# Attention stage of a fused attention and gated-MLP kernel: maxima in bursts next to P times V, a longer lag of ScalarE behind VectorE, and v copied by one engine

## The chip, the cores and the metric

The kernel runs on one core of one Trainium2 chip. The metric is the device time of one execution in microseconds; of the kernel before there are three runs, with a median of 1105.15 us (1102.87 to 1105.18). One further execution was profiled; it took 1106.79 us, 1.6 us over that median. A core has a matrix engine (TensorE; PE in the profile, with its weight loads listed as PEld), VectorE (DVE), ScalarE (ACT), GpSimd (POOL), and SyncE (SP), which here only starts DMA transfers. Each engine works through its own instructions in order and waits on semaphores for the others.

## The reference

One layer norm feeds two branches, and both are added to the input. The first branch is causal attention with 32 heads of 20 columns and a sliding window of 256 keys over 2048 tokens; the second is a gated MLP with 1728 hidden columns.

```python
xn = layernorm(x)                                  # 2048 x 640
q, k, v = split(xn @ wqkv)                         # 32 heads x 20
s = (q @ k.T) * 20 ** -0.5                         # masked: 0 <= row - col < 256
attn = softmax(s) @ v @ wo
mlp = (gelu_tanh(xn @ w_gate) * (xn @ w_up)) @ w_down
out = x + attn + mlp
```

## The kernel before

All dense products are made from numbers that are split in a high and a low part, three matrix multiplications for one (`dense_steps`, L100 to L106). The program has three stages. In the first one the layer norm is computed and x is transposed. In the second one, `attention()` (L753), all of the attention is computed while dense products run between its parts. The third stage holds the rest of the gate and up products and the down and output projections; the change does not touch it.

The attention stage has 32 units: 8 groups of 4 heads times 4 chunks of 512 query rows (`u = g * 4 + c`). Each unit has 14 slots, and `now[0]` counts slots. The order in which the five engines get their work is written out by hand in that loop (a manual schedule for PE, ACT, DVE and POOL); only the order of the SP queue, which starts most DMAs, is left to the framework. Within a unit these parts are issued:

- Eight calls of `max_pair` (L456). A call computes 128 query rows against up to 384 keys for two heads at once; the two heads use two halves of the rows of the matrix engine and write two PSUM banks (`ps_m`, tag `mx`). VectorE then reduces each bank to row maxima (L475). A burst is `pull_max(2, T)`: two calls, four banks, four reductions. The bursts run ahead: with twelve calls made before unit 0, a burst in unit u works for unit u+1 or u+2. `MXD` slots after the last call of a unit, `max_end` (L489) transposes the maxima (`ps_n`) and sends them to the q tile as two further rows.
- Twelve calls of `exp_piece` (L516): scores of one head into a bank of the pool `psx` (`ps_e`, tag `ex`, two banks), which ScalarE turns into exponentials `P` (L532). Two calls are made every other slot. After each fourth call POOL clears the corners outside of the mask (`clear`, L536).
- One call of `av_unit` for the unit before (L549): P times v for four heads in four column groups of the matrix engine, 1536 columns for each head and 1152 in chunk 0, into one bank (`ps_o`) that ScalarE copies to `ob` (L561).
- In slot 12, `load_stack(u + 3)` (L442): twelve DMAs that bring the q and k of a later unit.
- In every slot, `pull_fill(RATE / NS)`: 42.2 / 14 = 3.01 dense matmuls as fill between the rest. They make the q and k projections (`proj_qk`), the v projections (`proj_v`), and six tiles of the gated MLP (`gate_up_fill`), one after another.

A projection that has ended is taken out of its PSUM bank in steps, each deferred by slots (`defer`). For q and k (`save_qk`): ScalarE copies the high part (`upper`), VectorE subtracts (`middle`, L254), ScalarE copies the rest (`lower`, L239), POOL subtracts once more (L240), and a slot later SP stores. For the MLP: `c1` (ACT), `c2` (DVE, L610), `c3` (ACT, tanh, L614), `c4` and `c5` (DVE), and a store. VectorE steps of this kind go through `late()`: they are collected, and `flush()` issues them behind the other work of the slot. For v (`save_v`, L307): four copies from one bank, two by ScalarE and two by VectorE in turn while the attention loop runs.

PSUM has eight banks: two for fill (`psd`), two for scores (`psx`), and four (`psm`) for maxima, `ps_n`, and, before the change, `ps_o`.

Of the kernel before, what the change touches and what calls it, by code (L numbers as in the profile page):

```python
# [9 lines left out]
F32 = mybir.dt.float32  # L10
F32R = mybir.dt.float32r
BF = mybir.dt.bfloat16
AF = mybir.ActivationFunctionType
# [6 lines left out]
C = 512  # L20
# [10 lines left out]
NS = 14  # L31
RATE = 42.2
V1_SLOT = 158
MXD = 6
BURSTS = 1, 5, 9, 13
NFA = 6
HD = D // 2
HR = 5
# [26 lines left out]
def block_kernel(ctx, tc, x, wqk, wv, wgu, wdo, wdl, out):  # L65
    nc = tc.nc
# [65 lines left out]
    psx = pp.enter_context(tc.tile_pool(name="psx", bufs=2, space=PSUM))  # L132
    psm = pp.enter_context(tc.tile_pool(name="psm", bufs=4, space=PSUM))
# [71 lines left out]
    def flush():  # L205
        while lates:
            fn, a = lates.pop(0)
            fn(*a)

    def defer(n, fn, *a):  # L210
        if now[0] is None:
            fn(*a)
        else:
            at(now[0] + n, fn, *a)
# [17 lines left out]
    def save_qk(t, c, ps):  # L232
        pt = qkp.tile([128, 3, C], BF, name="pt", tag="pt")
        r = qkp.tile([128, C], F32, name="r", tag="r", bufs=1)
        dst = (qd if t < 5 else kd)[c]
        h, l = (2, 0) if t < 5 else (0, 2)

        def lower():
            nc.scalar.activation(pt[:, 1, :], r, AF.Copy)  # L239
            nc.gpsimd.tensor_tensor(out=pt[:, l, :], in0=r, in1=pt[:, 1, :], op=OP.subtract)  # L240
            defer(1, store)

        def store():
            a, end = t % 5 * 128, t % 5 * 128 + 128
            while a < end:
                g, b = divmod(a, 4 * DH)
                n = min(4 * DH - b, end - a)
                p = n - end + a + 128
                nc.sync.dma_start(dst[g, :, b:b + n, :].rearrange("p m t -> m p t"), pt[p - n:p])
                a += n  # L250
            done.add((t, c))

        def middle():
            nc.vector.tensor_tensor(out=r, in0=ps, in1=pt[:, h, :], op=OP.subtract)  # L254
            defer(1 if now[0] is None or now[0] < NS else 2, lower)

        def upper():
            nc.scalar.activation(pt[:, h, :], ps, AF.Copy)
            late(middle)

        defer(1, upper)
# [45 lines left out]
    def save_v(ps, vt, t):  # L307
        done.update((id(v), t) for v in vt)
        for g in range(4):
            o = vt[g][:, t * 84:(t + 1) * 84].rearrange("p (j d) -> p j d", d=21)[:, :, 0:20]  # L310
            i = ps[:, g * 80:(g + 1) * 80].rearrange("p (j d) -> p j d", d=20)
            if g % 2 and now[0] is not None:
                nc.vector.tensor_copy(o, i)  # L313
            else:
                nc.scalar.activation(o, i, AF.Copy)

    def run(*gens):
        for gen in gens:
# [197 lines left out]
    def exp_piece(u, s):  # L516
        g, c = divmod(u, NC)
        bi, j = divmod(s, 4)
        bank = pieces(c)[bi]
        q = qs[u % NQ]  # L520
        if j == 0:
            pts[u, bi] = ap.tile([128, 4, C], F32, name="P", tag="P", bufs=3)
        pt = pts[u, bi]
        lo = min(p[1] for p in bank)
        hi = max(p[1] + p[3] for p in bank)
        ps = psx.tile([128, C], F32, name="ps_e", tag="ex")
        for kb, col, q0, n in sorted(bank, key=lambda p: p[3]):
            k = ks[(u - (kb < 4 * c)) % NK]
            kc = kb % 4 * 128
            nc.tensor.matmul(ps[:, col:col + n], k[0:QROWS, j, kc:kc + 128], q[0:QROWS, j, q0:q0 + n],  # L530
                             start=True, stop=True)
        nc.scalar.activation(pt[:, j, lo:hi], ps[:, lo:hi], AF.Exp, scale=SCALE)  # L532
        if j == 3:
            defer(1, clear, u, bi)
# [13 lines left out]

    def av_unit(u):  # L549
        g, c = divmod(u, NC)  # L550
        o, v = psm.tile([128, C], F32, name="ps_o", tag="mx"), vtiles[g]
        todo = [(pts[u, bi], *p) for bi, bank in enumerate(pieces(c)) for p in bank]
        for i, (pt, kb, col, q0, n) in enumerate(todo):
            assert (id(v), kb) in done, (u, kb)
            for j in range(4):
                w0_ = kb * 84 + 21 * j
                nc.tensor.matmul(o[32 * j:32 * j + 32, q0:q0 + n], v[:, w0_:w0_ + 32], pt[:, j, col:col + n],  # L557
                                 start=i == 0, stop=i == len(todo) - 1, skip_group_check=True,
                                 tile_position=(0, 32 * j))
        ob = ap.tile([128, C], F32, name="ob", tag="ob", bufs=1)  # L560
        nc.scalar.activation(ob, o, AF.Copy)  # L561

        def store():
            for j in range(4):
                nc.sync.dma_start(od[c].rearrange("(d h) t -> h d t", h=H)[4 * g + j], ob[32 * j:32 * j + DH, :])
            nc.sync.dma_start(sd[c][4 * g:4 * g + 4, :], ob[DH::32, :])

        defer(3, store)
# [27 lines left out]
    def gate_up_fill(f, ws, c):  # L596
        cs = slice(c * C, (c + 1) * C)
        pss = []
        st = {}

        def c1():
            gs = st["g"] = hp.tile([128, C], F32, name="gs", tag="gs")
            t = st["t"] = hp.tile([128, C], F32, name="he", tag="he", bufs=2)
            nc.scalar.activation(gs, pss[0], AF.Copy)
            nc.scalar.activation(t, pss[0], AF.Square, scale=math.sqrt(0.044715))
            defer(1, late, c2)

        def c2():
            gs, t = st["g"], st["t"]
            nc.vector.scalar_tensor_tensor(t, t, 1.0, gs, op0=OP.add, op1=OP.mult)  # L610
            defer(2, c3)

        def c3():
            nc.scalar.activation(st["t"], st["t"], AF.Tanh, scale=math.sqrt(2.0 / math.pi))  # L614
            defer(1, late, c4)

        def c4():
            nc.vector.scalar_tensor_tensor(st["g"], st["t"], 1.0, st["g"], op0=OP.add, op1=OP.mult)
            st["done"] = True

        def c5():
            if "done" not in st:
                defer(1, late, c5)
                return
            nc.vector.scalar_tensor_tensor(st["t"], st["g"], 0.5, pss[1], op0=OP.mult, op1=OP.mult)
            defer(1, lambda: nc.sync.dma_start(hd[f][c], st["t"]))

        for i, (wh, wl) in enumerate(ws):
            ps = psd.tile([128, C], F32, name="ps_d", tag="dn")
            pss.append(ps)  # L630
            yield from dense_steps(ps, lambda k: wh[:, k, :], lambda k: wl[:, k, :],
                                   lambda k: xh[:, k, cs], lambda k: xl[:, k, cs], KT)
            defer(1, *((late, c5) if i else (c1,)))
# [101 lines left out]
    def pull_max(n, slot):  # L735
        for _ in range(n):
            x = next(stream, None)
            if x is None:
                return
            max_pair(*x)  # L740
            if x[1] == 7:
                at(slot + (MXD if slot >= 0 else 4), max_end, x[0])
# [10 lines left out]
    def attention():  # L753
        now[0] = -1
        load_stack(0)
        load_stack(1)
        load_stack(2)
        for i, (p, k, half) in enumerate((p, k, half) for p in range(NC // 2) for k in range(2) for half in range(2)):
            for j, fn in enumerate(x_sums(p, k, half)):
                at(XS0 + XSN * i + 2 * j, fn)  # L760
        for i in range(12):
            now[0] = i - 13
            for fn, a in tick():
                fn(*a)
            if i % 2 == 0:
                pull_max(2, now[0])
            flush()
            pull_fill(2 * RAMP)
        pull_fill(GAP)
        for u in range(NU + 1):  # L770
            for i in range(NS):
                T = now[0] = NS * u + i
                for fn, a in tick():
                    fn(*a)
                if i == 0 and u:
                    av_unit(u - 1)
                if i % 2 and i < 12 and u < NU:
                    exp_piece(u, i - 1)
                    exp_piece(u, i)
                if i in BURSTS:  # L780
                    pull_max(2, T)
                flush()
                if i == 12 and 3 <= u + 3 < NU:
                    load_stack(u + 3)
                pull_fill(RATE / NS)
        while acts:
            now[0] += 1
            for fn, a in tick():
                fn(*a)
            flush()  # L790
        now[0] = None
        run(fill)
        assert not acts
# [651 lines left out]
```

## Time and profile before

| what | us |
|---|---|
| median of three runs | 1105.15 |
| profiled execution, whole | 1106.79 |
| its span on the core | 1105.0 |
| before unit 0 begins, about | 95 |
| units 0 to 31 and the last P times V | 579 |
| the rest | 431 |
| TensorE busy over the span | 1075.9 |
| VectorE busy over the span | 755.6 |
| ScalarE busy over the span | 512.6 |

The middle three rows are stretches of the profiled span (0 to 95, 95 to 674 and 674 to 1105 us). Busy time of TensorE counts modelled durations that overlap, so for TensorE the starts of its instructions say more than the busy share: in a row of the timeline the first column is the start of a merged group, and the difference to the start of the next row is what the group really took. The idle time in brackets is what was left after the modelled end.

### The profile page before, as it was taken

The numbers are of one execution on the slowest core, as the hardware profiler recorded it, in microseconds if no ns is written. First come the engines' busy times: TensorE is split into PE (matmuls) and PEld (weight loads), VectorE is DVE, ScalarE is ACT, GpSimd is POOL, SyncE is SP. The second block draws the span as 40 slices with busy tenths as digits, with TensorE's granted clock in tenths as the row PEclk, the third lists the DMA queues.
The fourth block names the chain that finished last, engine by engine and source line by source line (L and its number), as shares of the span: only waits on it lengthen the run. The fifth ranks groups of instructions, "written<-read, shape, count | busy, mean of one in ns | idle before, by whom it ended". The sixth has DMA issues, their size and how long they took to land.

```text
span 1105.0 us, 21154 instructions
## 1 busy us (share of the span) xinstructions
PE 1075.9 (97%) x7253; PEld 823.8 (75%) x7253; DVE 755.6 (68%) x2033; ACT 512.6 (46%) x1040; POOL 335.8 (30%) x514
## 2 busy tenths in 40 slices
PE   8999999999999999999999999999999999999998
PEld 7977565556666756666656657888888999999998
DVE  7755566556565556676666744777776869888887
ACT  4434565556544455546455556422323544433332
POOL 5022563557653265535436322111110000000000
PEclk9999999999999999999999999999999999999999
DMA  5552343454543244243424214457666883344443
GB/s 205 169 157 64 98 142 96 127 149 142 166 124 91 67 119 147 91 132 96 128 78 130 90 45 151 161 207 257 230 206 238 296 277 102 121 136 127 133 132 107
DMA packets 105171, 158.45 MB, mean 143 GB/s; under 512 B 15420, under 2 KB 60092, under 8 KB 105064
## 3 DMA queue, kind: packets, MB, share of 16 engines
q1 hardware_dynamic: 102680, 150.95, 43.0%
q10 hardware_dynamic: 2384, 6.16, 1.7%
q8 instruction: 57, 0.93, 0.4%
q14 instruction: 50, 0.41, 0.1%
HBM read 101.78 MB, written 54.92 MB: 142 GB/s over the span
## 4 chain that ended last, share of the span: by engine, by line
PE 59%; DVE 5%; ACT 2%; issue 1%; DMA 1%; POOL 1%; ACTq 0%; SPq 0%; DVEq 0%; POOLq 0%
PE ps_g L894 16%; PE ps L1161 15%; PE ps_d L104 14%; PE ps_o L557 5%; PE ps_e L530 4%; PE ps_m L471 2%; PE ps_v L104 2%; PE ps_g L104 1%; DVE junk L475 1%; DMA hr<-hd 1%; DVE at L999 1%; DVE ss L999 1%; DVE wb L999 1%; DVE wt L999 1%; ACT P L532 1%
## 5 line engine op out<-in xcount | busy, mean ns | idle before, releaser
L475 DVE CUSTOM_DVE_ANT_0 junk<-ps_m,mask 128x384 bf16<-128x384 f32 (+2 forms) x512 | 272.7, 533 | 190.0 <-PE ps_m L471 133.5
L532 ACT ACTIVATE P<-ps_e 128x512 f32<-128x512 f32 (+2 forms) x384 | 197.8, 569 | 68.0 <-PE ps_e L530 66.2
L1161 PE MATMUL ps<-wb,at 128*128 128x320 f32 x999 | 157.0, 310 | 2.2 <-DVE at L999 1.3
L1161 PEld LDWEIGHTS ps<-wb,at 128*128 128x128 f32 x999 | 148.9, 188 | 3.6 <-DVE at L999 1.8
L543 POOL TENSOR_SCALAR_AFFINE_SELECT P<-P 128x512 f32<-128x512 f32 x128 | 85.6, 669 | 183.3 <-ACT P L532 173.4
L104 PE MATMUL ps_d<-xh,wql 128*128 128x512 f32 x430 | 132.7, 416 | 0.0
L104 PE MATMUL ps_d<-xh,wqh 128*128 128x512 f32 x430 | 131.1, 414 | 0.8 <-DVE v L313 0.8
L104 PE MATMUL ps_d<-xl,wqh 128*128 128x512 f32 x430 | 131.2, 412 | 0.0
L530 PE MATMUL ps_e<-qs,ks 124*128 124x128 bf16 (+2 forms) x704 | 113.7, 277 | 10.5 <-ACT P L532 9.3
L104 PEld LDWEIGHTS ps_d<-xh,wqh 128*128 128x128 f32 x430 | 76.7, 189 | 28.4 <-issue 13.6
L104 PEld LDWEIGHTS ps_d<-xh,wql 128*128 128x128 f32 x430 | 77.5, 190 | 25.7 <-issue 13.0
L104 PEld LDWEIGHTS ps_d<-xl,wqh 128*128 128x128 f32 x430 | 77.6, 189 | 25.4 <-issue 12.6
L530 PEld LDWEIGHTS <-ks 124*128 124x128 bf16 x704 | 50.9, 98 | 60.6 <-issue 47.2
L1161 PE MATMUL ps<-wt,at 128*128 128x320 f32 x552 | 89.2, 310 | 0.8 <-DVE xr L1184 0.8
L557 PE MATMUL ps_o<-P,v 128*32 128x384 f32 (+2 forms) x1408 | 84.5, 386 | 2.0 <-DVE mx L475 1.0
L1161 PEld LDWEIGHTS ps<-wt,at 128*128 128x128 f32 x552 | 82.9, 188 | 1.3 <-DVE xr L1184 1.0
L546 POOL TENSOR_SCALAR_AFFINE_SELECT P<-P 128x512 f32<-128x512 f32 x112 | 71.2, 646 | 27.2 <-ACT P L532 27.2
L240 POOL TENSOR_TENSOR pt<-r,pt 128x512 bf16<-128x512 f32 x40 | 46.5, 1163 | 106.7 <-ACT pt L239 104.3
L1115 ACT ACTIVATE at<-ss 128x512 fp32r<-128x512 f32 x59 | 37.3, 632 | 88.7 <-DVE ss L999 88.7
L557 PEld LDWEIGHTS ps_o<-P,v 128*32 128x32 f32 x1408 | 40.6, 110 | 41.8 <-issue 26.9
L561 ACT ACTIVATE ob<-ps_o 128x512 f32<-128x512 f32 x32 | 19.1, 598 | 102.5 <-PE ps_o L557 71.9
L471 PE MATMUL ps_m<-ks,qs 60*128 60x128 bf16 (+1 forms) x704 | 63.5, 275 | 1.9 <-DVE xl L188 1.0
(190 smaller groups left out, 1687.3 us busy)
## 6 DMA issues: line engine op xcount, KB each, us to landing
hr<-hd SPq DMA_DIRECT2D x104, 128.0 KB
hd<-he SPq DMA_DIRECT2D x50, 256.0 KB
wr<-wgu SPq DMA_DIRECT2D x27, 320.0 KB
qs<-qd SPq DMA_DIRECT2D x64, 120.0 KB
ks<-kd SPq DMA_DIRECT2D x64, 120.0 KB
xi<-x SPq DMA_DIRECT2D x16, 320.0 KB
qs<-qd SPq DMA_DIRECT2D x64, 80.0 KB
ks<-kd SPq DMA_DIRECT2D x64, 80.0 KB
```

The lines of the kernel that those rows point to most:

```text
L104: nc.tensor.matmul(ps, a(k), b(k), start=n == 0, stop=n == 3 * nk - 1)
L240: nc.gpsimd.tensor_tensor(out=pt[:, l, :], in0=r, in1=pt[:, 1, :], op=OP.subtract)
L471: nc.tensor.matmul(ps[:, lo:hi], q[rows, j, 128 * b:128 * b + 128], kt[rows, j, k0:k1], start=True, stop=True, tile_position=(64 * r, 0))
L475: nc.vector.tensor_tensor_reduce(out=junk[:, 0:n], in0=ps[:, 0:n], in1=mask[:, 384 - n:384], scale=1.0, scalar=NEG, op0=OP.add, op1=OP.max ...
L530: nc.tensor.matmul(ps[:, col:col + n], k[0:QROWS, j, kc:kc + 128], q[0:QROWS, j, q0:q0 + n], start=True, stop=True)
L532: nc.scalar.activation(pt[:, j, lo:hi], ps[:, lo:hi], AF.Exp, scale=SCALE)
L543: nc.gpsimd.affine_select(out=a, in_=a, pattern=[[0, 4], [1, 128]], compare_op=OP.is_ge, fill=0.0, base=0, channel_multiplier=-1)
L546: nc.gpsimd.affine_select(out=a, in_=a, pattern=[[0, 4], [-1, 128]], compare_op=OP.is_ge, fill=0.0, base=-1, channel_multiplier=1)
L557: nc.tensor.matmul(o[32 * j:32 * j + 32, q0:q0 + n], v[:, w0_:w0_ + 32], pt[:, j, col:col + n], start=i == 0, stop=i == len(todo) - 1, ski ...
L894: nc.tensor.matmul(ps, i, j, start=first and n == 0, stop=n == len(work) - 1, skip_group_check=True)
L999: nc.vector.tensor_tensor(out=o, in0=i, in1=j, op=op)
L1161: nc.tensor.matmul(ps[bank][:, 0:HD], *work[bank][j], start=bank not in begun, stop=final[p, bank] == n and j == len(work[bank]) - 1, skip ...
```

## The change

Four things change in the attention loop.

- The bursts move from slots 1, 5, 9 and 13, behind the scores of the slot, to slots 0, 4 and 8, ahead of them. Slot 0 has two bursts, one ahead of `av_unit` and one behind it, with a `flush()` between. In unit 0, which has no `av_unit`, the second burst is in slot 2.
- The scores move from the odd slots 1 to 11 to the even slots 0 to 10.
- `ps_o` moves from the pool `psm` to `psx`, and so takes a turn with the banks of the scores.
- `lower` follows `middle`, and `c3` follows `c2`, by `LAG = 4` slots and no longer by 2. The four copies of `save_v` are all made by ScalarE.

```diff
-BURSTS = 1, 5, 9, 13
+LAG = 4
...
         def middle():
             nc.vector.tensor_tensor(out=r, in0=ps, in1=pt[:, h, :], op=OP.subtract)
-            defer(1 if now[0] is None or now[0] < NS else 2, lower)
+            defer(1 if now[0] is None or now[0] < NS else LAG, lower)
...
-            if g % 2 and now[0] is not None:
-                nc.vector.tensor_copy(o, i)
-            else:
-                nc.scalar.activation(o, i, AF.Copy)
+            nc.scalar.activation(o, i, AF.Copy)
...
-        o, v = psm.tile([128, C], F32, name="ps_o", tag="mx"), vtiles[g]
+        o, v = psx.tile([128, C], F32, name="ps_o", tag="ex"), vtiles[g]
...
-            defer(2, c3)
+            defer(LAG, c3)
...
+                if i in (0, 4, 8) or T == 2:
+                    pull_max(2, T)
                 if i == 0 and u:
                     av_unit(u - 1)
-                if i % 2 and i < 12 and u < NU:
-                    exp_piece(u, i - 1)
+                    flush()
+                    pull_max(2, T)
+                if i % 2 == 0 and i < 12 and u < NU:
                     exp_piece(u, i)
-                if i in BURSTS:
-                    pull_max(2, T)
+                    exp_piece(u, i + 1)
                 flush()
```

## The prediction

> **What bounds the kernel now.** I read the busy shares by stretch first, then the waits of TensorE and of ScalarE, and then the timeline of TensorE row by row.
>
> ```profile
> span 1105.0 us, 21154 instructions
> ```
>
> ```profile
> 95.00:674.00 579.00, 563.59 (x4267) 357.68 (x4265) 351.11 (x1178) 312.51 (x643) 290.24 (x460) 1.00 0.37 111
> 674.00:1105.00 431.00, 424.66 (x2440) 390.19 (x2432) 342.31 (x669) 163.50 (x294) 19.05 (x13) 1.00 0.55 183
> ```
>
> The columns are the stretch, busy time of PE, PEld, DVE, ACT and POOL, granted clock, DMA share, GB/s. In the attention stretch PE is busy for 563.6 of 579 us at full clock, DVE for 351 (61%), ACT for 313: TensorE bounds it. It can only get shorter by stalls that go away and by matmuls that take less time. The second stretch is not edited and I take it as it is.
>
> ```profile
> PE ps_e L530 <- ACT P L532: 9.3, 13, 0.9
> PE ps_v L104 <- DVE v L313: 2.4, 3, 1.1
> PE ps_d L104 <- DVE v L313: 0.8, 1, 0.8
> ```
>
> ```profile
> ACT pt L239 <- DVE r L254: 26.0, 22, 2.8
> ACT he L614 <- DVE he L610: 20.6, 13, 3.1
> ```
>
> These are us in total, times, longest. Nearly all that PE waits for here are score banks which ScalarE has not emptied, and v banks. The next rows, three engines in one stretch, show why.
>
> ```profile
> 118.66 0.56 DVE L475 CUSTOM_DVE_ANT_0 junk<-ps_m,mask 128x384 bf16<-128x384 f32 x1 [1.62 <-PE ps_m L471]
> ...
> 119.36 0.56 DVE L475 CUSTOM_DVE_ANT_0 junk<-ps_m,mask 128x384 bf16<-128x384 f32 x1
> ...
> 121.13 1.08 PE L104 MATMUL ps_d<-xl,wqh 128*128 128x512 f32 x4
> 121.27 0.69 DVE L254 TENSOR_TENSOR r<-ps_d,pt 128x512 f32<-128x512 f32 x1
> ...
> 121.99 0.63 ACT L239 ACTIVATE pt<-r 128x512 bf16<-128x512 f32 x1 [2.31 <-DVE r L254]
> 122.52 2.19 ACT L532 ACTIVATE P<-ps_e 128x512 f32<-128x512 f32 x4
> 123.15 0.86 PE L530 MATMUL ps_e<-qs,ks 124*128 124x256 bf16 x4 [0.95 <-ACT P L532]
> 123.95 0.52 PE L471 MATMUL ps_m<-ks,qs 60*128 60x128 bf16 x8
> 124.32 0.56 DVE L475 CUSTOM_DVE_ANT_0 junk<-ps_m,mask 128x384 bf16<-128x384 f32 x1 [2.08 <-PE ps_m L471]
> 124.40 0.50 PE L104 MATMUL ps_d<-xl,wqh 128*128 128x512 f32 x1
> ```
>
> Four reductions, 0.71 us apart (118.66 to 119.36), hold DVE for 2.8 us; `middle` (L254) stands behind them. `lower` (L239) comes two slots later at the head of ACT's queue, waits 2.31 us for `middle`, and behind it stand the exponentials, so PE waits for a score bank.
>
> **Prices on TensorE**, from starts:
>
> ```profile
> 415.86 0.61 PE L530 MATMUL ps_e<-qs,ks 124*128 124x128 bf16 x4
> 416.17 1.00 PE L104 MATMUL ps_d<-xh,wqh 128*128 128x512 f32 x3
> 417.01 0.85 PE L104 MATMUL ps_d<-xh,wql 128*128 128x512 f32 x3
> 417.70 0.61 PE L530 MATMUL ps_e<-qs,ks 124*128 124x256 bf16 x4
> 418.24 0.50 PE L471 MATMUL ps_m<-ks,qs 60*128 60x128 bf16 x8
> 418.68 0.73 PE L104 MATMUL ps_d<-xh,wql 128*128 128x512 f32 x2
> 419.25 1.09 PE L104 MATMUL ps_d<-xl,wqh 128*128 128x512 f32 x4
> ...
> 420.92 1.33 PE L104 MATMUL ps_d<-xh,wqh 128*128 128x512 f32 x5
> 422.17 0.50 PE L471 MATMUL ps_m<-ks,qs 60*128 60x384 bf16 x4
> 422.60 0.96 PE L104 MATMUL ps_d<-xh,wql 128*128 128x512 f32 x3
> 423.75 2.80 PE L557 MATMUL ps_o<-P,v 128*32 128x384 f32 x48 [0.19 <-DVE mx L475]
> 426.48 0.73 PE L104 MATMUL ps_d<-xh,wql 128*128 128x512 f32 x2
> 427.05 0.40 PE L104 MATMUL ps_d<-xl,wqh 128*128 128x512 f32 x1
> ```
>
> - One fill matmul takes 0.23 us (three from 417.01 to 417.70).
> - Two scores take 0.31 us to the next fill, which then has 0.15 us more than three times 0.23: 0.46 in all. That is 0.45 ns for each of 1024 columns, the rate of the fill: entering and leaving scores is free.
> - A burst costs 0.10 us ahead (five fills took 1.25 and not 1.15), 0.43 itself, and 0.11 behind (two fills took 0.57): 0.64. Its 768 columns (two pairs, each side by side) stream in 0.35 at that rate. So 0.29 is entry (0.10) and exit (0.19). Behind scores it costs no less: 417.70 to 418.68 and 0.11 is 1.09, minus 0.46 is 0.63.
> - P times v takes 2.73 and 0.11 behind it; its entry, not readable beside the 0.19 of idle time, I take as 0.10.
>
> **The change, part by part.**
>
> *Order on PE.* Before, a unit has five such passages (four bursts and P times v) with an entry and an exit each: 5 x 0.29 = 1.45 us. After, slot 0 has one entry, burst to P times v (a), P times v to burst (b), and an exit to scores (c); slots 4 and 8 each an entry and an exit to scores. That is 0.30 + a + b + 3c. None of the three stands in the trace. For c, the exit to fill is the bound above (0.19); it has 0.08 ahead of the fill and 0.11 behind its first matmul, and 0.08 alone is the bound below; 0.15, between them, since scores leave for free otherwise. For a and b, the bounds are nothing and a whole exit and entry (0.29); the nearest row is the entry alone, 0.10. So 0.95, and 0.50 saved per unit; 0.45 taken. Full bursts fall in 30 units: **-14 us**, between 0 and -27.
>
> The row has 0.10 in and 0.19 out of each passage. The Trainium skill, "TensorEngine Tiling (Array Packing)", Key Properties, says that changing the tiling mode drains TensorE. The two heads of a burst and the four of P times v are different modes, so by that rule a and b are whole changes and this term is near its small end; the rival of cheap joins below is that case.
>
> *LAG.* For about 30 q and k projections `lower`, its subtraction on POOL and two or three stores on SP come two slots later; for 24 gate tiles c3 comes two slots later, and c4, c5 and the store one. Two slots hold six fills and two scores, 6 x 0.23 + 0.46 = 1.84 us, more than the 1.36 that PE lost in the stretch above (worked out next). So both ACT rows above should nearly vanish, and the 13 PE waits with them. Their price is more than the 0.72 of idle time: from 121.13 to 123.15 four fills took 2.02 and not 0.93, and scores and burst (123.15 to 124.40) 1.25 and not 0.98, so 1.36 there. At 1.15 each: **-15 us** (-10 to -18). What it costs: `middle` writes `r` again one slot after `lower` of the set before (sets are 15 / 3.01 = 5 slots apart), so DVE may wait for POOL. That is covered by the idle part of DVE except where it falls into slots 12 and 13, ahead of the maxima.
>
> *v by ACT alone.*
>
> ```profile
> L315 ACT ACTIVATE v<-ps_v 128x80 f32<-128x80 f32 x80 | 16.4, 241 | 45.5 <-DVE v L313 26.5 <-PE ps_v L104 18.7 <-issue 0.2
> L313 DVE COPY v<-ps_v 128x80 f32<-128x80 f32 x48 | 11.4, 240 | 15.3 <-ACT v L315 15.2
> ```
>
> The two engines alternate and wait for each other. 48 copies of 0.24 move: 11.4 us more on ACT, which loses 26.5 of waiting. The four PE waits (3.2 us, with refill about 4) go; new ones behind exponentials cost perhaps 1: **-3 us** (0 to -4).
>
> *ps_o in psx.* ACT's copy frees the bank about 0.7 us after P times v; the burst behind it and the first score take 0.43 + 0.23. Nothing, or 0.1 x 31 at the worst.
>
> *New waits in slot 0.* The second burst needs the four banks of the first. Its reductions begin 0.37 after the burst (123.95 to 124.32): 0.10 + 0.37 + 4 x 0.71 = 3.31 us after the slot begins. PE gets to the last two banks at 0.10 + 0.43 + 2.73 + 0.17 = 3.43: just hidden. In eight units P times v is short (1152 of 1536 columns, 0.68 less), and PE waits about 0.55: **+4 us**. Where a VectorE step of slot 13 comes late, the wait is up to 0.7; seven such units: **+4 us** for this and the `r` case (0 to 20; the upper end is one step of 0.69 in each of 30 units).
>
> *Loads.* A unit's q and k are loaded from slot 12 on; the first maxima that need them stood 11 slots later and now 6. From the prices, slots 0 to 3 take 4.84, 0.69, 1.15 and 0.69: slot 4 begins 7.4 us after slot 0, 6.8 after P times v starts.
>
> ```profile
> 276.13 1.07 PE L557 MATMUL ps_o<-P,v 128*32 128x384 f32 x16
> ```
>
> ```profile
> 441.54 0.16 PEld L557 LDWEIGHTS ps_o<-P,v 128*32 128x32 f32 x8 [0.36 <-POOL P L543]
> ```
>
> ```profile
> 277.20 3.29 SPq L450 DMA_DIRECT2D qs<-qd  x6
> 280.53 2.21 SPq L450 DMA_DIRECT2D ks<-kd  x6
> ...
> 439.99 3.00 SPq L450 DMA_DIRECT2D ks<-kd  x6
> ```
>
> ```profile
> 0.81 1.82 SPq L137 DMA_DIRECT2D xi<-x  x4
> 3.98 0.49 DVE L142 BATCH_NORM_STATS2 st<-xi 128x6 f32<-128x320 f32 x1 [2.86 <-DMA xi<-x]
> ```
>
> At the program's start a transfer was usable 3.2 us after its issue began, which I use as flight. The last of the six issues from 280.53 begins at about 282.4 and then lands at 285.6, 9.5 us after P times v began at 276.13: 2.7 late for slot 4. Most units are like the other one: its last issue begins at about 442.6 and lands at 445.8, 4.3 us after P times v began at 441.54 and 2.5 early. With four or five late units of 30, taken as missing by 1 us each, as the scores end a slot earlier and free the q tile for the load: **+4 us** (0 to 30).
>
> Sum: -14 - 15 - 3 + 4 + 4 + 4 = -20 us. The span of 1105.0 would be about 1085; against the profiled execution 1106.8 that is 1087, against the median, 1.6 lower, **1085**. 0.2% (2.2 us) is about what a measurement can tell from no change.
>
> **The rivals.**
>
> - *Joins are not cheap* (a and b 0.29 each, c 0.15): the order saves 0.12 x 30 = 4 us and no longer 14, so 1095. For it: each change of shape that the trace shows costs. Against: the 0.19 of an exit is partly the fill's own weight load, which neither join has. 0.17.
> - *VectorE becomes late*: eight reductions (5.7 us) stand in slot 0 of a unit that is to take 17.5, and 0.69 late in every unit costs 30 x 0.69 = 21 and not 4: 1102. For it: 16 reductions of 0.71 and 4.2 MLP steps of 0.69 are 14.3 of 17.5 us. Against: slots 9 to 13 have none of the maxima, and five slots of fill to catch up. 0.10.
> - *The loads bind* (slower): the place is the first weight load of the burst in slot 4, which waits for twelve DMAs. In the order of the SP queue of the changed program a store that waits for POOL or VectorE stands between the twelve in 18 units, against 7 before. Each microsecond by which an average unit's loads miss slot 4 costs 30. The rest of the sum is -24, so it decides from 0.8 us on; at 1.1 it gives 1114. For it: one unit as quoted misses by 2.7. Against: these stores belong to slots before 13, and the typical unit has 2.5 us to spare. 0.13.
> - *The lag does nothing*, since ACT then waits in other places: 15 us less gain, 1100. Only where DVE is over 4 slots late, which the second rival has: within its chance.
>
> **How the numbers follow.** The sum has 0.60, with a range of its own from 1071 (joins free, loads in time) to 1096. With 0.17, 0.10 and 0.13 for the three rivals, 1066 to 1107 leaves out the loads' case and the far ends. Faster: 0.60 + 0.17 and half of the second, 0.82 less 0.02 for ends = 0.80; within 0.2%: 0.05; slower: 0.13 and 0.02.
>
> **What would show it.** In the profile after, the last P times v starts near 651 and no longer at 671. The PE waits for `P` fall under 3 us, ACT's waits for `r` and `he` under 10 together. A start-to-start reading of slot 0 gives a, b and c. The order is wrong if burst, P times v, burst and two scores take over 4.9 us without a wait; the loads' rival is right if the weight load of L468 waits for q or k DMAs for over 10 us; VectorE's if PE waits for `mx` or `junk` for over 15.

## The result and the profile after

The changed kernel takes **1079.51 us** (median of 4, 1077.33 to 1081.88) against 1105.16 for the kernel before beside it (1102.87 to 1107.01): a ratio of 0.977, interval 0.974 to 0.980, 25.6 us less. It was forecast faster, at 1085. The profiled execution took 1078.76 us.

Three marks divide the gain in the two profiled spans (1105.0 and 1076.7). The first P times v starts at 110.53 before and at 107.74 after, 2.8 earlier. From the first to the last P times v it is 561.0 us before and 537.0 after; I call this **the loop**, and it lost 24.0. What follows the last P times v was 433.5 and is 431.9. Of the first 2.8, 1.7 is a clock dip that fell into the profile of before alone (last section).

The span and the attention stretch of after, by windows (columns as in the prediction):

```profile
span 1076.7 us, 21130 instructions
95.00:653.00 558.00, 547.91 (x4269) 365.02 (x4269) 346.60 (x1141) 315.76 (x684) 287.78 (x461) 1.00 0.39 116
```

TensorE still bounds the attention stretch, at full clock. Its waits from 60 to 676 us (us in total, times, longest):

```profile
PE ps_d L104 <- DVE he L622: 3.3, 6, 0.9
PE ps_m L468 <- DVE mx L472: 2.4, 7, 0.4
PE ps_m L468 <- DMA ks<-kd: 2.2, 3, 1.3
...
PE ps_e L527 <- ACT P L529: 0.9, 1, 0.9
PE ps_e L527 <- ACT ob L558: 0.4, 1, 0.4
```

The waits for `P` fell from 9.3 us to 0.9, and those for v are gone. The first row is new: 3.3 us for `he`, which `c5` (L622) reads out of a fill bank. The waits of ScalarE for VectorE shrank, and VectorE waits for POOL instead:

```profile
ACT pt L239 <- DVE r L254: 3.5, 4, 1.2
ACT he L611 <- DVE he L607: 1.7, 3, 0.7
```

```profile
DVE r L254 <- POOL pt L240: 26.0, 14, 4.3
```

Slot 0 and slot 8 of one unit on TensorE's timeline:

```profile
404.18 0.84 PE L104 MATMUL ps_d<-xh,wql 128*128 128x512 f32 x3
404.95 0.50 PE L468 MATMUL ps_m<-ks,qs 60*128 60x128 bf16 x8
405.39 2.80 PE L554 MATMUL ps_o<-P,v 128*32 128x384 f32 x48
408.12 0.57 PE L468 MATMUL ps_m<-ks,qs 60*128 60x384 bf16 x4
408.62 0.65 PE L527 MATMUL ps_e<-qs,ks 124*128 124x128 bf16 x4
408.98 0.77 PE L104 MATMUL ps_d<-xh,wql 128*128 128x512 f32 x2
409.59 1.07 PE L104 MATMUL ps_d<-xl,wqh 128*128 128x512 f32 x4
...
415.97 0.61 PE L104 MATMUL ps_d<-xh,wqh 128*128 128x512 f32 x2
416.52 0.50 PE L468 MATMUL ps_m<-ks,qs 60*128 60x384 bf16 x4
416.95 0.61 PE L527 MATMUL ps_e<-qs,ks 124*128 124x256 bf16 x4
417.32 0.94 PE L104 MATMUL ps_d<-xh,wqh 128*128 128x512 f32 x3
418.09 0.85 PE L104 MATMUL ps_d<-xh,wql 128*128 128x512 f32 x3
```

From starts, with 0.233 a fill: slot 0's group takes 4.03 (404.95 to 408.98), 0.07 of entry ahead of it (three fills in 0.77) and 0.14 behind it (two fills in 0.61): about 4.25. The same work before was, by the prediction's prices, a burst alone (0.64), P times v (2.94) and a burst with scores (1.09): 4.67. Slot 8 takes 0.80, and 0.08 and 0.07 at its ends: 0.95 against 1.09; with slot 4 that is 0.24 to 0.28 a unit. Together some 0.65 a unit, or 19.5 us in 30 units, an estimate from these prices. The idle time listed for the loop fell by 4.6 us: before, 9.3 for `P`, 1.2 for v and 2.6 in three other rows make 13.1, and the rows above, without two of the waits for `mx` that lie ahead of the loop (0.7), make 8.5.

Both together are 24.1, but that this is just the 24 of the loop is luck, since the list does not hold all that TensorE loses. In the eight units whose P times v is short, the second burst waits for the reductions of the first:

```profile
458.89 0.56 DVE L472 CUSTOM_DVE_ANT_0 junk<-ps_m,mask 128x384 bf16<-128x384 f32 x1
458.90 0.93 PE L468 MATMUL ps_m<-ks,qs 60*128 60x384 bf16 x4
...
459.76 0.61 PE L527 MATMUL ps_e<-qs,ks 124*128 124x128 bf16 x4
```

The fourth reduction ends at 459.45, and the burst takes 0.86 (458.90 to 459.76) where the one in slot 8 takes 0.43. That is 0.43 in each of eight units, 3.4 us in all, and the list has almost none of it. So some 3 us of the gain are not assigned: a stall costs more than its listed idle time, as the prediction found for one.

### The profile page after: what moved, and what is told of

The parts are those of the page before. It is cut to its first block, busy times and chain, and to the rows that moved or that the text cites. A ratio compares the mean times of both kernels' runs of the same rounds, so it can differ in the third digit from the quotient of the medians.

```text
span 1076.7 us, 21130 instructions
## 1 busy us (share of the span) xinstructions
PE 1055.0 (98%) x7253; PEld 827.3 (77%) x7253; DVE 746.9 (69%) x1985; ACT 516.1 (48%) x1088; POOL 332.6 (31%) x514
## 4 chain that ended last, share of the span: by engine, by line
PE 79%; DVE 8%; DMA 4%; POOL 3%; issue 3%; ACT 2%; SPq 1%; ACTq 0%; DVEq 0%; POOLq 0%
PE ps_d L104 23%; PE ps L1160 16%; PE ps_g L893 15%; PE ps_e L527 7%; PE ps_v L104 6%; PE ps_o L554 6%; PE ps_m L468 4%; DVE junk L472 2%; PE ps_g L104 1%; POOL pt L240 1%; DVE ss L998 1%; DVE at L998 1%; DMA hr<-od 1%; PE ps_t L179 1%; DMA qs<-qd 1%
## 5 line engine op out<-in xcount | busy, mean ns | idle before, releaser
L104 PE MATMUL ps_d<-xh,wqh 128*128 128x512 f32 x430 | 127.2, 409 | 3.3 <-DVE he L622 3.3
L104 PE MATMUL ps_d<-xh,wql 128*128 128x512 f32 x430 | 126.8, 408 | 0.0
L104 PE MATMUL ps_d<-xl,wqh 128*128 128x512 f32 x430 | 126.4, 406 | 0.0
L468 PE MATMUL ps_m<-ks,qs 60*128 60x128 bf16 (+1 forms) x704 | 67.6, 275 | 6.5 <-DVE mx L472 2.4
```

The source lines that it names most:

```text
L104: nc.tensor.matmul(ps, a(k), b(k), start=n == 0, stop=n == 3 * nk - 1)
L468: nc.tensor.matmul(ps[:, lo:hi], q[rows, j, 128 * b:128 * b + 128], kt[rows, j, k0:k1], start=True, stop=True, tile_position=(64 * r, 0))
```

## The experiments

All times are medians beside runs of the kernel before on the same chip (1104.8 to 1106.1); "loop" is from the first to the last P times v in the profile.

| run | us | ratio, interval | loop |
|---|---|---|---|
| before | 1105.2 | 1 | 561.0 |
| the change | 1079.5 | 0.977 (0.974 to 0.980) | 537.0 |
| e1_lag_only | 1100.0 | 0.9955 (0.994 to 0.997) | 555.9 |
| e2_order_only | 1076.4 | 0.975 (0.972 to 0.978) | 533.0 |
| e3_v_only | 1097.8 | 0.993 (0.991 to 0.995) | 556.4 |
| e4_after_lag2 | 1074.0 | 0.972 (0.970 to 0.974) | 531.4 |
| e7_after_psm | 1109.9 | 1.0035 (1.002 to 1.005) | 568.9 |
| e8_after_c3lag2 | 1073.3 | 0.970 (0.969 to 0.972) | 532.0 |
| e10_before_ahead | 1083.7 | 0.979 (0.977 to 0.981) | 539.8 |
| e11_lag2_load10 | 1069.6 | 0.967 (0.966 to 0.969) | 528.1 |
| e12_short_split | 1081.2 | 0.979 (0.977 to 0.980) | 538.2 |
| e13_before_lower4 | 1099.0 | 0.9945 (0.992 to 0.997) | 554.2 |
| e14_lag2_split | 1115.5 | 1.009 (1.008 to 1.011) | 572.2 |

The loop of e2 holds one stretch at a lower granted clock (0.77 from 152.5 to 160 us, which is 1.7 us of work), and that of e7 holds two; without it, e2's loop is 531.3.

### The parts alone: e1, e2, e3, e4

The first theory is the prediction's: the order and the lag each bring about 15 us. Each part alone tells.

**e1: the lag in the kernel before.**

```diff
-            defer(1 if now[0] is None or now[0] < NS else 2, lower)
+            defer(1 if now[0] is None or now[0] < NS else LAG, lower)
...
-            defer(2, c3)
+            defer(LAG, c3)
```

> The kernel before with the lag of four slots alone (lower behind middle, c3 behind c2). If the parts add up, the 13 waits of TensorE for P and ScalarE's waits for r and he go, and the time falls by 10 to 15 us, to 1090 to 1095. If the lag matters only with the new order, where eight reductions stand in one slot, it falls by less than 5 us.

The lag alone brought 5 us and not 15. The profile's waits of TensorE say why:

```profile
PE ps_d L105 <- DVE he L626: 6.6, 6, 1.4
...
PE ps_e L531 <- ACT P L533: 1.7, 4, 0.8
```

The waits for `P` went, as forecast, from 9.3 to 1.7. But 6.6 us of waits for `he` came, which the kernel before did not have.

**e2: the order alone** (bursts, scores, `ps_o` in `psx`), with the lag of 2 and v copied by both engines; the edit is against the changed kernel.

```diff
-            defer(1 if now[0] is None or now[0] < NS else LAG, lower)
+            defer(1 if now[0] is None or now[0] < NS else 2, lower)
...
-            nc.scalar.activation(o, i, AF.Copy)
+            if g % 2 and now[0] is not None:
+                nc.vector.tensor_copy(o, i)
+            else:
+                nc.scalar.activation(o, i, AF.Copy)
...
-            defer(LAG, c3)
+            defer(2, c3)
```

> The new order alone (bursts in slots 0, 4, 8, scores in even slots, ps_o in psx), with the lag of two slots and v copied by two engines. If the parts add up, the fewer changes of shape save 17 us and new waits in slots 0 and 4 cost about 8: 1094 to 1099, with TensorE's waits for P about as before (13 of them). If the order depends on the lag, eight reductions ahead of middle make ScalarE wait longer than before and the time is 1105 or more.

The order alone gives 1076.4, no less than the whole change: the intervals overlap, and its loop is 4.0 us shorter. TensorE's waits for `P`, and then ScalarE's for VectorE:

```profile
PE ps_e L530 <- ACT P L532: 0.3, 2, 0.2
```

```profile
ACT pt L239 <- DVE r L254: 15.8, 15, 2.3
ACT he L614 <- DVE he L610: 7.6, 8, 2.1
```

With the lag of 2, ScalarE still waits 23 us for VectorE, but TensorE waits 0.3 us for `P`. So these waits of ScalarE are not what has to go.

**e3: v by ScalarE alone, in the kernel before.**

```diff
-            if g % 2 and now[0] is not None:
-                nc.vector.tensor_copy(o, i)
-            else:
-                nc.scalar.activation(o, i, AF.Copy)
+            nc.scalar.activation(o, i, AF.Copy)
```

> The kernel before with v copied by ScalarE alone. As predicted: the waits of TensorE for the v banks (3.2 us) go, 3 to 4 us less, 1101 to 1102. The rival: the copies are now behind exponentials in ScalarE's queue and nothing is gained, 1104 to 1106.

It brought 7.6 us by the ratio (7.0 by the medians); 4.6 of it stands in the loop, where the listed waits for v had been 1.2 us.

**e4: the changed kernel with `LAG` = 2.**

```diff
-LAG = 4
+LAG = 2
```

> The changed kernel with the lag put back to two slots. If the parts add up, 12 to 15 us slower than the changed kernel, 1091 to 1095. If the new order needs the lag, over 20 us slower, 1100 or more.

It is 5.5 us *faster* than the change, where it was expected slower. So with the new order the lag costs 5.5 us. From e2 to e4 only v differs: 2.4 us by the medians, which is within the spread of e2's runs (1073.6 to 1082.8), and nothing in the loop (531.3 without the stretch at a lower clock, and 531.4). The parts don't add: alone they brought 5, 28 and 7.6.

### Which part of the order: e10

The new theory was that the place of the bursts ahead of the scores carries most, and the joins with P times v the rest. e10 is the kernel before with only the two blocks of the slot exchanged; bursts stay in slots 1, 5, 9 and 13.

```diff
+                if i in BURSTS:
+                    pull_max(2, T)
                 if i % 2 and i < 12 and u < NU:
                     exp_piece(u, i - 1)
                     exp_piece(u, i)
-                if i in BURSTS:
-                    pull_max(2, T)
```

> The kernel before with its four bursts moved ahead of the scores of the same slots, and nothing else. If it is the place ahead of the scores that takes away TensorE's waits for P (reductions begin 0.46 us earlier, the next scores stand 0.5 us later), these waits fall from 13 to 4 or fewer, 8 to 12 us, and leaving a burst to scores in place of fill saves 3 x 0.075 x 30 = 7 us: 1086 to 1090. If the waits go only because slots with bursts are fewer or because the maxima stand next to P times v, they stay, and the time is 1097 to 1100.

An exchange of two blocks brings 22 us, 21.2 of it in the loop. Timeline and waits of TensorE:

```profile
415.25 0.84 PE L104 MATMUL ps_d<-xh,wql 128*128 128x512 f32 x3
416.02 0.50 PE L471 MATMUL ps_m<-ks,qs 60*128 60x384 bf16 x4
...
416.77 0.77 PE L104 MATMUL ps_d<-xh,wql 128*128 128x512 f32 x2
417.37 0.85 PE L104 MATMUL ps_d<-xl,wqh 128*128 128x512 f32 x3
```

```profile
PE ps_e L530 <- ACT P L532: 2.2, 8, 0.6
```

Burst and scores take 0.07 + 0.75 + 0.13 = 0.95 in this order and 1.09 in the other. At three such groups a unit that is 0.14 x 3 x 30 = 12.6 us (from one P times v to the next, an undisturbed unit went from 17.78 to 17.44, which makes it 10); the waits listed in the loop fell by some 9, to 5. Both together are about the 21. From e10 to e2 the loop loses another 6.8, or 8.5 without e2's stretch at a lower clock: the joins beside P times v, with `ps_o` in `psx`.

Why the waits for `P` shrank stands in the place that the prediction shows before (118.66 to 123.15), here in e10:

```profile
116.87 0.56 DVE L475 CUSTOM_DVE_ANT_0 junk<-ps_m,mask 128x384 bf16<-128x384 f32 x1 [1.50 <-PE ps_m L471]
...
121.37 0.87 PE L530 MATMUL ps_e<-qs,ks 124*128 124x256 bf16 x4 [0.18 <-ACT P L532]
```

From the first reduction to the scores that wait it is 4.50 us here and was 4.49 before, so the chain of reductions, `middle`, `lower` and exponentials is as long as it was. But TensorE is ready for these scores 4.32 us after that reduction (121.37 less 0.18) and no longer 3.54 (123.15 less 0.95): the burst and its reductions come earlier, and the next burst now stands ahead of the scores that wait. Before, eight of the 13 waits were of 0.94 or 0.95 us; here all eight are at 0.18 to 0.61.

### Which half of the lag costs: e8, e13

**e8: the change, with only `c3` back at 2.**

```diff
-            defer(LAG, c3)
+            defer(2, c3)
```

> The changed kernel with c3 two slots behind c2 again, and lower still four behind middle. If the cost of the lag is that c5 frees the PSUM bank of the up product a slot later, TensorE's waits for he (3.3 us, 6 of them) go and the time is 1074.5 to 1076.5, most of the way to the 1074.0 of the lag of two. If the cost is VectorE's wait for POOL before it writes r again (26 us on VectorE), the time stays at 1078 to 1080.

It gives back all that the lag cost in sum: 1073.3, as e4. Its waits of TensorE, and then of VectorE:

```profile
PE ps_m L468 <- DVE mx L472: 3.8, 11, 0.5
```

```profile
DVE r L254 <- POOL pt L240: 24.9, 13, 4.0
```

No wait for `he` is left. VectorE's 25 us of waiting for POOL, which the late `lower` brings, are all still there. Most of them show no cost, but in three units `middle` stands ahead of the reductions of slot 0 and makes them late. In the changed kernel, where P times v of such a unit starts at 266.75:

```profile
267.21 0.69 DVE L254 TENSOR_TENSOR r<-ps_d,pt 128x512 f32<-128x512 f32 x1 [4.33 <-POOL pt L240]
...
270.80 0.61 PE L527 MATMUL ps_e<-qs,ks 124*128 124x128 bf16 x4
```

The scores come 4.05 us after the start of P times v; in the other full units it is 3.16 to 3.29. By the start of the fill behind them, these three units lose 0.8, 0.9 and 1.3 us in the changed kernel, 3.0 in all, and 1.7, 1.0 and 1.3 in e8, 4.1 in all; e4 has none of it. That e8 is no slower than e4 comes from another side: e4 waits for loads in two of the same units, and such waits for transfers fell from 4.7 us in e4 to 1.7 in e8.

The path of the other half stands in three rows of VectorE and one of TensorE, in the changed kernel:

```profile
604.64 0.56 DVE L472 CUSTOM_DVE_ANT_0 junk<-ps_m,mask 128x384 bf16<-128x384 f32 x1
...
605.12 0.69 DVE L615 SCALAR_TENSOR_TENSOR gs<-he,gs 128x512 f32<-128x512 f32 x1
605.84 0.69 DVE L622 SCALAR_TENSOR_TENSOR he<-gs,ps_d 128x512 f32<-128x512 f32 x1
...
606.59 0.50 PE L104 MATMUL ps_d<-xh,wqh 128*128 128x512 f32 x1 [0.35 <-DVE he L622]
```

`c4` (L615) and `c5` (L622) stand behind reductions, and `c5` is what frees the bank of the up product; the next fill tile has to have that bank.

**e13: the kernel before, with the lag of 4 for `lower` alone.**

```diff
-            defer(1 if now[0] is None or now[0] < NS else 2, lower)
+            defer(1 if now[0] is None or now[0] < NS else 4, lower)
```

> The kernel before with lower four slots behind middle, and c3 still two behind c2. If the side cost of the lag is all in c3, as the run with c3 put back says, the waits for P that come from projections go (about 8 of 13) and no waits for he come: 1094 to 1097, better than the 1100 of both lags. If the cost is on lower's side too, 1099 to 1102.

```profile
PE ps_e L530 <- ACT P L532: 5.5, 8, 0.9
```

At 1099.0 it misses the 1094 to 1097 of the forecast and lies at the near end of the other case, a cost on `lower`'s side too. No wait for `he` came, and VectorE waits 3.2 us for POOL before it writes `r`; whether that is the cost, no run shows. `lower` alone takes 5 of the 13 waits and brings 6 us. With `c3` as well (e1) 7.6 us of waits for `P` go, yet the time is no better: what `c3` takes off ScalarE it puts on the fill bank.

### What stands beside P times v: e7, e14, e12

**e7: the change with `ps_o` back among the banks of the maxima.**

```diff
-        o, v = psx.tile([128, C], F32, name="ps_o", tag="ex"), vtiles[g]
+        o, v = psm.tile([128, C], F32, name="ps_o", tag="mx"), vtiles[g]
```

> The changed kernel with ps_o back in the pool of the maxima (psm). If the separate pool is what lets the second burst stand next to P times v, then ps_o waits for the first reduction (about 0.6 us a unit) and the last bank of the second burst waits for the copy of ps_o (about 0.7 us): 20 to 40 us slower than the changed kernel, 1100 to 1120. If the pool is of no account, 1078 to 1082.

```profile
PE ps_o L554 <- DVE mx L472: 20.5, 27, 2.6
```

The change with this one line as it was would be slower than the kernel before. P times v then waits for a reduction of the burst just ahead of it, and the second burst for ScalarE's copy of `ps_o` (8.7 us in 30 waits).

**e14: e4, with the second burst of slot 0 moved to slot 2 in every unit.**

```diff
-                if i in (0, 4, 8) or T == 2:
+                if i in (0, 2, 4, 8):
...
                     flush()
-                    pull_max(2, T)
```

> The changed kernel with a lag of two slots (1074.0) and the second burst of slot 0 moved to slot 2 in every unit, so that P times v stands between a burst and two scores. By the prices read from the changed kernel (0.095 us for each entry and each join, 0.115 for an exit to scores) one more exit costs 3 to 4 us, and eight waits of 0.4 us fall away: 1073 to 1075.5. If standing next to P times v is worth what the prediction had (14 us with the place ahead of the scores), 1079 or more.

It lost 41.6 us against e4, 40.8 of it in the loop; neither price explains that. The timeline of TensorE in one unit, and its waits:

```profile
425.59 0.50 PE L468 MATMUL ps_m<-ks,qs 60*128 60x128 bf16 x8
...
429.54 0.38 PE L527 MATMUL ps_e<-qs,ks 124*128 124x128 bf16 x2 [0.39 <-ACT ob L558]
429.62 0.76 PE L104 MATMUL ps_d<-xh,wql 128*128 128x512 f32 x2
...
439.32 0.32 PE L468 MATMUL ps_m<-ks,qs 60*128 60x384 bf16 x1 [0.45 <-ACT mr L491]
```

```profile
PE ps_m L468 <- DVE mx L472: 14.2, 36, 0.5
PE ps_e L527 <- ACT ob L558: 12.7, 31, 0.4
PE ps_m L468 <- ACT mr L491: 5.3, 10, 1.2
```

From the burst to the fill it is 4.03 us (425.59 to 429.62), to the hundredth what the changed kernel takes there *with* the second burst (404.95 to 408.98). Without that burst, the second score waits for ScalarE's copy of `ps_o`. So in slot 0 the second burst of a full unit is free (where P times v is short, the fill starts 0.28 later with it), and in slot 2 it is paid: 0.5 in a full unit. Its four reductions, two slots ahead of the next burst, are not done when that one wants the banks: from the burst of slot 4 to that of slot 8 it takes 0.6 to 0.8 longer in most units. And since the last call for a unit now comes in slot 2, `max_end` moves from slot 6 to slot 8, right ahead of a burst: `ps_n` takes one of the four banks, and the burst waits until ScalarE has copied it to `mr`. From slot 8 to the next unit it takes 0.24 to 1.2 longer. By starts, these three stretches lose 10.5, 15.2 and 14.6 us against e4 in the 29 units that have bursts in all of them, 40.2 of the 40.8.

**e12: e11 (below), with the second burst moved to slot 2 only in the eight units where P times v is short.**

```diff
-                if i in (0, 4, 8) or T == 2:
+                if i in (0, 4, 8) or i == 2 and u % NC == 1 or T == 2:
...
                     flush()
-                    pull_max(2, T)
+                    if u % NC != 1:
+                        pull_max(2, T)
```

> The changed kernel with a lag of two slots, loads in slot 10, and the second burst of slot 0 moved to slot 2 in the eight units whose P times v is short. If TensorE's wait of about 0.4 us in these units is what the last 1.4 us of waits for the maxima and the longer slot 0 there cost, less one more entry and exit (0.1 us a unit), 2 to 3 us less than with the loads alone: 1066.5 to 1068. If the wait only moves, 1069 to 1071.

It missed the forecast by 13 us and is 11.6 slower than e11, 10.1 of it in the loop. The three costs are those of e14: by starts against e11, the loop loses 2.1 us up to the burst of slot 4, 4.2 from there to that of slot 8, and 3.8 from slot 8 on, 10.1 in all. The list of waits shows 6.2 of it, for `mx` (4.3, and 1.4 in e11) and for `ob` (3.7, and 0.4).

### The loads: e11

e4, with the loads of a unit's q and k issued from slot 10.

```diff
-                if i == 12 and 3 <= u + 3 < NU:
+                if i == 10 and 3 <= u + 3 < NU:
```

> The changed kernel with a lag of two slots and the loads of q and k issued in slot 10 in place of slot 12, right behind the last scores that read the tiles. If late loads are what the first burst of slot 4 still waits for, TensorE's waits there (3.8 us with the lag of two) go: 1069 to 1071.5. If the loads are held up by the stores ahead of them in SP's queue and not by their slot, nothing changes: 1073 to 1075.

```profile
PE ps_m L468 <- DVE mx L472: 1.4, 4, 0.5
```

4.4 us less than e4, whose `ps_m` waits for transfers were 4.7 us in total (for `ks`, which is loaded, and for the stores to `kd` and `qd` that the loads follow) and are 1.7 here. This is the fastest version, **1069.59 us** (1069.30 to 1071.03), 0.9% under the changed kernel.

## Why the prediction was right, and where it was not

The forecast came out: 1085 against 1079.5. That the sum came so near is luck in good part: the lag's 15 us did not come, and the order brought about twice what it was given.

**Order on PE: the mechanism was right, the size too small** (-14 forecast, -19.5 by the prices above). c, the exit to scores, was taken as 0.15 and is 0.06 to 0.08 (slot 8: 0.95 less 0.46 of scores, 0.35 of streaming and 0.08 of entry). a is 0.09 (burst to P times v 0.44, for 0.35 of streaming), as taken. P times v to burst is 2.73 as before, and the 0.11 behind it is gone. A price for b can't be told apart: the second burst takes 0.43 in most full units, as one beside fill, and 0.50 in the one shown. The first rival, joins at a full exit and entry, is out, and with it the prediction's strict reading of the Trainium skill's "TensorEngine Tiling (Array Packing)", Key Properties, that a change of the tiling mode drains TensorE: each change does cost here, but the join that shows costs 0.09, an entry, and not 0.29. What the term left out is that the order also takes away TensorE's waits for `P`.

**LAG: this step failed.** The prediction had TensorE's 13 waits down to ScalarE waiting for VectorE, and concluded that with a later ScalarE "both ACT rows should nearly vanish, and the 13 PE waits with them" (-15). They do go that way: from 9.3 us to 1.7 in e1. But with the new order they are gone without the lag (e2), although ScalarE still waits for VectorE half as long as before (23 us of 47). The step took it that TensorE waits as long as ScalarE waits for VectorE. It passed over when TensorE gets to the scores: e10 shows the same chain of 4.5 us, with TensorE ready for the scores 0.78 later against it, and the wait down from 0.95 to 0.18. For the scores in even slots (e2) no such pair of rows was taken, and that it is the same there is argued. The sentence on what the lag costs counted the late `r`, rightly (3.0 us in three units, below), but passed over "c4, c5 and the store one" slot later: `c5` holds a bank that the fill wants. In the new order that makes the lag +5.5 us, not -15.

**v**: forecast -3 with up to -4. Alone it brought 7.6; in the new order 2.4 by the medians, not clear of noise. The listed waits (3.2 us with those ahead of the loop) were only part of what the two engines' copies cost in the old order; what the rest was stays open.

**ps_o in psx, "nothing"**: nearer to its worst case. The list has 0.4 us in one wait, but from the scores of slot 0 to the fill it is 0.43 in a full unit (476.95 to 477.38) and 0.31 in a short one (459.76 to 460.07), whose copy ends before the first score. In a full unit the copy ends at 3.46 and the second score begins at 3.51 us after the start of P times v, with the second burst as without it (e14). That is 0.12 in each of some 20 units, about 2.5 us. The step named what hides the copy, the burst and the first score; e14 shows the listed price without the burst, 12.7 us.

**New waits in slot 0**: +8 forecast, and some 6.4 by starts, though the list has only 1.7 for `mx` in the loop. The short units lose 0.43 each, 3.4 in all (forecast 0.55 each, +4). The late VectorE step costs 3.0 in three units (forecast +4 in seven), through the `r` case that the step named. The second rival had this mechanism, and lacks the size: three units, not thirty.

**Loads**: +4 forecast; 2.2 listed, and 4.4 gained where they start earlier (e11). The rival of the loads had its mechanism right and lacks the size: three waits in two late units, not thirty.

Of the signs named: the last P times v starts at 644.8 (forecast 651), the waits for `P` are 0.9 (under 3), ScalarE's two waits 5.2 together (under 10), slot 0's group 4.03 (under 4.9), waits for q and k 2.2 (under 10), for `mx` 2.4 (under 15). All hold, and yet two of them, read as proof of the lag, would have misled: the waits for `P` fell because of the order, and ScalarE's waits, which the lag did shorten (23 us in e4), were by then worth nothing. Working forward from the runs: order -28 (e2), v -2.4 (e2 to e4, not clear of noise), lag +5.5 (e4 to the change): -25 of the 25.6.

## What to carry to other kernels

A wait that vanishes from the bound engine need not have been cured by the part that was meant for it: run each part alone and each part taken out, and let the lists of waits say which one did it. The lists miss short stalls, so compare the starts of undisturbed units too: 0.43 us in each of eight units was all but absent from them. When a step is deferred, look up which bank or buffer the end of its chain gives back, since that is where the next stall comes from. Where two shapes of matmul must alternate on TensorE, their order within a slot is worth pricing from starts: exchanging two blocks of the loop's code brought 22 us here.

## What the runs showed of the hardware that was not expected

What a small-tile group costs at its ends depends on its neighbour. Behind it, a 128 x 512 fp32 fill costs 0.19, scores in bf16 0.06 to 0.08, and another small-tile shape 0.09.

The granted clock dips in the prologue in some executions and not in others. Windows of before, and then of the changed kernel:

```profile
60.00:62.50 2.50, 1.27 (x10) 0.62 (x8) 2.48 (x5) 2.13 (x5) 1.16 (x1) 1.00 0.46 143
62.50:65.00 2.50, 2.47 (x8) 1.79 (x8) 1.94 (x9) 0.00 (x0) 0.00 (x0) 0.68 0.77 220
65.00:67.50 2.50, 2.50 (x9) 1.99 (x8) 0.00 (x0) 0.00 (x0) 0.00 (x0) 0.64 0.65 199
```

```profile
60.00:62.50 2.50, 1.43 (x11) 0.78 (x10) 2.48 (x5) 2.29 (x5) 1.16 (x1) 1.00 0.53 159
62.50:65.00 2.50, 2.31 (x10) 1.78 (x10) 2.10 (x10) 0.00 (x0) 0.00 (x0) 1.00 0.70 204
```

In both, TensorE is about half idle from 60 to 62.5 us; only in the first does the clock fall after it, by 2.5 x (0.32 + 0.36) = 1.7 us of work, or some 3.4 us at half speed. The same dip stands in six of the thirteen profiles. The Trainium skill, "TensorE: Matmul & The Clock Gate", Part 1, has a gate that halves the clock by the activity in free-running windows of about 3.4 us, so that the phase decides; the length here agrees with it. TensorE was not idle for all of such a window here: it was about half busy, and the longest listed wait in it is 1.04 us. For reading a trace it means that 1.7 us between two profiles can be this alone, and that the loop, at full clock in all of them but e2 and e7, is the better measure.
